# A gated attention and MLP kernel: the first block's projections as plain fp32 products

## The chip, the core and the metric

The kernel runs on one core of one Trainium2 chip. The core has five engines that work at the same time, each through its own list of instructions in order: TensorE (PE, with its weight loads shown as PEld), VectorE (DVE), ScalarE (ACT), GpSimd (POOL) and SyncE (SP, which here only issues transfers). They wait for each other through semaphores. The metric is the device time of one execution in microseconds (us). Three runs before the change took 1068.99, 1069.96 and 1070.19 us, so the median is 1069.96 us.

## The reference: what is computed

For 2048 tokens of width 448 the result is `g * a + (1 - g) * b`. The gate `g` is a sigmoid of one product per token. `a` is attention with 16 query heads of width 28 that share one key head and one value head. `b` is a two-part mixer: a layernorm, a product with `w1`, gelu, four groups of channels shifted by +1, -1, +2 and -2 tokens, a product with `w2` added to `x`, and then a second layernorm with an MLP through `w3` and `w4`.

```
q = (x @ wq).reshape(B, S, H, Dh).transpose(0, 2, 1, 3);  k = x @ wk;  v = x @ wv
p = softmax(einsum("bhqd,bkd->bhqk", q, k) * Dh ** -0.5);  a = merge(p @ v) @ wo
h = gelu(layernorm(x) @ w1);  x1 = x + shifted(h) @ w2
b = x1 + gelu(layernorm(x1) @ w3) @ w4
```

Everything is float32.

## The kernel before

The 448 channels are held as three chunks of 128 and one of 64 rows (`chunks` on the host also repeats the last 64 rows in the upper half of the fourth chunk). The 2048 tokens are four blocks of 512.

**Split products.** A float32 product on TensorE is written in this kernel as several products of a rounded type (`fp32r`, `F32R` in the code). Each operand `a` is split into `ah`, its rounded copy, and `al = a - ah`. `proj` then adds `wh*ah`, `wh*al` and `wl*ah` for three chunks; for the fourth, whose lower part fills the spare 64 rows, it adds two products: 11 matmuls of 512 columns for one output tile. `split_w` makes the two halves of a weight and `split_a` those of an activation: a copy on ACT and subtractions on DVE, or on POOL where `eng` says so.

**Stages.** Stage 1 (`s1`, up to about 105 us) makes keys and values of all blocks (`stage_kv`, `stage_v`), the queries of the first block's head groups 0 and 1 (`stage_q`), and the first half of the mixer (`ln1_begin` and `ln1_tile`, `stage_w1`, `stage_w2`). Stage 2 (up to about 425 us) is the MLP. Stage 3 is attention, bounded by exponentials on ACT together with TensorE, and the output product. The change touches stage 1 only.

**Layernorm.** `layernorm_stats` takes four DVE statistics (`bn_stats`, `bn_aggr`) of a block and then, on POOL, adds epsilon and raises to the power -0.5. `layernorm_tile` normalizes 128 tokens on DVE, repeats the last 64 channels with a POOL copy, transposes four 128x128 pieces on TensorE into one of two `tp` tiles, and splits the result with `split_a`.

**Order.** TensorE's order is that of the program text. The order on the other engines is found by a scheduler when the kernel is built, and is then fixed. Stage 1 begins with 30 small matmuls (`warm`) that only occupy TensorE, then keys and values of block 0, query group 0, the value transposes, query group 1, layernorm of block 0 and `stage_w1(0)`. `stage_w1(b)` has four steps `m` of 112 output channels; between them it transposes layernorm tiles of block `b+1`. Each step ends in two gelus on ACT and a subtraction on POOL (`hh`, `hf`, `hl`).

**Transfers.** SP issues the loads in order: block 0 of the transposed input (`xkv_0`, two halves), two groups of `wq`, block 0 of `x` (`x1`), `w1`, block 1 of `x`, `xkv_1`, `w2`, blocks 2 and 3 of `x`. The six copies of the first queries into their stacked tile (`qs`, `q_evac`) follow on the same queue. `xkv` tiles, `w1raw` and `w2raw` share three buffers (`raw`).

Of the kernel before, what the change touches and what calls it, by code (L numbers as in the profile page):

```python
# [15 lines left out]
P = 128  # L16
# [24 lines left out]
def gated_mix_kernel(  # L41
# [30 lines left out]
    gi = keep.tile([P, NT], F32, name="gi")  # L72
    epst = keep.tile([P, 4], F32, name="epst")
# [4 lines left out]
    nc.gpsimd.memset(powt, -0.5)  # L78
    nc.gpsimd.memset(vext, 0.0)
# [16 lines left out]
    for _ in range(30):  # L96
        nc.tensor.matmul(wps[:, 0:256], warm[:, 0:P], warm, start=True, stop=True)
# [22 lines left out]

    def layernorm_stats(pool, b):
        mv = pool.tile([P, 4, 2], F32, tag="mv", bufs=2, name=f"mv_{pool.name}_{b}")
        rs = pool.tile([P, 4], F32, tag="rs", bufs=2, name=f"rs_{pool.name}_{b}")
        for t in range(4):
            st = pool.tile([P, 6], F32, tag="st", bufs=4, name=f"st_{pool.name}_{b}_{t}")
            nc.vector.bn_stats(st, x1[:, 4 * b + t, :])
            nc.vector.bn_aggr(mv[:, t, :], st)
        nc.gpsimd.tensor_tensor(rs, mv[:, :, 1], epst, ALU.add)
        nc.gpsimd.tensor_tensor(rs, rs, powt, ALU.pow)
        return mv, rs  # L130

    def layernorm_tile(pool, tp_of, b, t, mv, rs, ah, al):
        xt = x1[:, 4 * b + t, :]
        xn = pool.tile([P, 512], F32, tag="xn", bufs=3, name=f"xn_{pool.name}_{b}_{t}")
        nc.vector.tensor_scalar(xn[:, 0:D], xt, mv[:, t, 0:1], rs[:, t:t + 1],
                                op0=ALU.subtract, op1=ALU.mult)
        nc.gpsimd.tensor_copy(xn[:, D:512], xn[:, 384:D])
        tp = tp_of(f"tp_{pool.name}_{b}_{t}").rearrange("p (c n) -> p c n", c=4)
        for c in range(4):
            nc.tensor.transpose(tp[:, c, :], xn[:, c * P:(c + 1) * P], ident)  # L140
        cols = slice(t * P, (t + 1) * P)
        split_a(tp, ah[:, :, cols], al[:, :, cols])
# [60 lines left out]
    with tc.tile_pool(name="s1b", bufs=1) as s1b, \  # L203
# [6 lines left out]
        xraw, xact = {}, {}  # L210
# [10 lines left out]
        nc.scalar.dma_start(kvraw, wkv)  # L221
        xraw[0] = s1.tile([P, 4, 512], F32, tag="raw", bufs=3, name="xkv_0")
        for c in (0, 2):
            nc.sync.dma_start(xraw[0][:, c:c + 2, :], xT[:, c:c + 2, 0:512])
        wqraw = s1.tile([P, 4, 256], F32, name="wq01raw")
        nc.sync.dma_start(wqraw, wq[:, :, 0:256])
        load_x1(0)
        w1raw = s1.tile([P, 4, 512], F32, tag="raw", bufs=3, name="w1raw")[:, :, 0:D]
        nc.sync.dma_start(w1raw, w1)
        load_x1(1)  # L230
        load_x(1)
        w2raw = s1.tile([P, 4, 512], F32, tag="raw", bufs=3, name="w2raw")[:, :, 0:D]
        nc.sync.dma_start(w2raw[0:C, :, :], w2.rearrange("(q p) n -> p q n", p=C))
        load_x1(2)
        load_x1(3)

# [6 lines left out]
        wqh = s1.tile([P, 4, 256], F32R, name="wq01h")  # L243
        wql = s1.tile([P, 4, 256], F32R, name="wq01l")
        hh, hl, acts = {}, {}, {}

        def stage_kv(b):
            ah = s1.tile([P, 4, 512], F32R, tag="ah", bufs=2, name=f"ahk_{b}")
            al = s1.tile([P, 3, 512], F32R, tag="al", bufs=2, name=f"alk_{b}")
            if b == 0:  # L250
                for c in range(4):
                    nc.scalar.copy(ah[:, c, :], xraw[b][:, c, :])
                    if c < 3:
                        nc.vector.tensor_sub(al[:, c, :], xraw[b][:, c, :], f32(ah)[:, c, :])
                    else:
                        nc.vector.tensor_sub(ah[64:128, c, :], xraw[b][64:128, c, :], f32(ah)[64:128, c, :])
            else:
                split_a(xraw[b], ah, al)
            xact[b] = (ah, al)
            cols = slice(512 * b, 512 * b + 512)  # L260
            ps = max_tile(f"kv_{b}")[0:64, :]
            proj(ps, kvh, kvl, ah, al)
            nc.scalar.copy(kS[0:32, cols], ps[0:32, :])
            nc.scalar.copy(kS[32:64, cols], ps[0:32, :])
            nc.vector.tensor_sub(kS[64:96, cols], ps[0:32, :], f32(kS)[0:32, cols])
            vT = s1b.tile([32, 512], F32, tag="vT", bufs=1, name=f"vT_{b}")
            nc.scalar.copy(vT, ps[32:64, :])
            return vT
# [9 lines left out]
        def stage_q(u):  # L278
            ps = mm_tile(f"q_{u}")
            proj(ps, wqh[:, :, u * P:(u + 1) * P], wql[:, :, u * P:(u + 1) * P], *xact[0])  # L280
            q_of[u] = keep.tile([P, 4, 512], F32R, name=f"qs_{u}", tag=f"qs{u}", bufs=1)
            q_evac(s1, u, ps, q_of[u])

        def ln1_begin(b):
            ah = s1.tile([P, 4, 512], F32R, tag="ah", bufs=2, name=f"ah1_{b}")
            al = s1.tile([P, 3, 512], F32R, tag="al", bufs=2, name=f"al1_{b}")
            acts[b] = (ah, al, *layernorm_stats(s1, b))
# [5 lines left out]
        def stage_w1(b):  # L293
# [4 lines left out]
            for m in range(4):  # L298
                ps = mm_tile(f"h_{b}_{m}")
                proj(ps[0:C, :], w1h[:, :, m * C:(m + 1) * C], w1l[:, :, m * C:(m + 1) * C], *acts[b][0:2])  # L300
                if b + 1 < NB:
                    ln1_tile(b + 1, m)
# [27 lines left out]
        split_w(kvraw, kvh, kvl)  # L330
        vT = stage_kv(0)
        split_w(wqraw, wqh, wql, nc.gpsimd)
# [6 lines left out]
        split_w(w1raw, w1h, w1l, nc.gpsimd)  # L339
        stage_w1(0)  # L340
        nc.scalar.copy(w2h[0:C], w2raw[0:C])
        nc.gpsimd.tensor_tensor(w2l[0:C], w2raw[0:C], f32(w2h)[0:C], ALU.subtract)
# [466 lines left out]
```

## Time and profile before

| | |
|---|---|
| median of three runs | 1069.96 us (1068.99 to 1070.19) |
| the profiled execution | 1067.96 us, of which 1066.2 us are the span of its instructions |
| TensorE busy | 1040.3 us (98%), 5610 records |
| ScalarE busy | 673.5 us (63%) |
| VectorE busy | 258.6 us (24%) |
| GpSimd busy | 146.1 us (14%) |
| chain that ended last | 92% TensorE, 2% VectorE, 2% transfers |

The profile shows one execution. Rows of the timeline have a start, a duration, an engine, a line of the kernel, the operation and its tiles, and in brackets how long the engine had been idle and who released it. A table of windows gives for each stretch of time the busy time of each engine with its number of instructions, then the granted TensorE clock as a share of full speed, the share of the transfer engines and GB/s. Matmuls overlap, so a busy TensorE is not TensorE at its peak. Tile names in the profile leave numbers out: `h` is an output of `stage_w1`, `kv` of `stage_kv`, `q` of `stage_q`, `tp_s` a transposed layernorm tile of stage 1, `al` and `ah` its two halves.

### The profile page before, as it was taken

Reading aid. Unit: us, or ns where it says so; the run is one execution under the profiler, and the core shown is the slowest. Engines: PE = TensorE matmul, PEld = TensorE weight load, DVE = VectorE, ACT = ScalarE, POOL = GpSimd, SP = SyncE. Lnnn points to the kernel's source line nnn. Section 1 sums busy time; section 2 is a strip of 40 time slices with the busy share of each in tenths; the row PEclk is TensorE's granted clock in tenths of the full one; section 3 lists DMA queues with packets and bytes.
Section 4 is the critical chain, followed back from the end, with each engine's and each line's share of the span. In section 5 each row is a group of like instructions: output and inputs, shape, how many; then the busy total and the mean of one; then the engine's idle time right before and its main releaser. Section 6 shows DMA issues by size and latency. Waiting matters only on the chain.

```text
span 1066.2 us, 13945 instructions
## 1 busy us (share of the span) xinstructions
PE 1040.3 (98%) x5610; PEld 679.5 (64%) x5610; DVE 258.6 (24%) x528; ACT 673.5 (63%) x1318; POOL 146.1 (14%) x175
## 2 busy tenths in 40 slices
PE   7999989999999999999999999999999999999996
PEld 4787878888888887454554555554655555555442
DVE  6734862411412212301110110120110210111102
ACT  5444462222222223798888888889888888888873
POOL 5622200200200202602000002020002010000100
PEclk8899999999999999999999999999999999999998
DMA  9501330000000001323211202220202220202001
GB/s 312 133 1 37 112 111 1 1 1 1 1 1 1 1 1 61 132 32 70 32 18 15 31 19 41 39 31 3 39 10 41 39 31 2 40 21 30 10 2 38
DMA packets 30541, 41.15 MB, mean 39 GB/s; under 512 B 8004, under 2 KB 20100, under 8 KB 30340
## 3 DMA queue, kind: packets, MB, share of 16 engines
q1 hardware_dynamic: 30324, 40.04, 16.2%
q8 instruction: 46, 0.75, 0.3%
q14 instruction: 27, 0.22, 0.1%
q10 hardware_dynamic: 144, 0.13, 0.0%
HBM read 23.28 MB, written 3.67 MB: 25 GB/s over the span
## 4 chain that ended last, share of the span: by engine, by line
PE 92%; DVE 2%; DMA 2%; ACT 1%; POOL 1%; issue 1%; SPq 0%; POOLq 0%; DVEq 0%; ACTq 0%
PE s L662 27%; PE pv L624 22%; PE acc L418 4%; PE acc L419 4%; PE acc L420 4%; PE g L115 4%; PE g L116 4%; PE g L117 4%; PE q L502 3%; PE m L166 2%; PE wo L559 1%; PE wo L557 1%; PE g L119 1%; PE wo L555 1%; PE g L118 1%; PE h L116 1%
## 5 line engine op out<-in xcount | busy, mean ns | idle before, releaser
L664 ACT ACTIVATE p<-s 128x512 f32<-128x512 f32 x1024 | 517.6, 630 | 99.7 <-PE s L662 99.4
L662 PE MATMUL s<-qs,kS 98*128 98x512 f32 x1024 | 343.5, 420 | 1.4 <-ACT p L664 0.7
L662 PEld LDWEIGHTS s<-qs,kS 98*128 98x128 f32 x1024 | 181.7, 189 | 168.3 <-ACT p L664 126.2
L624 PE MATMUL pv<-p,vext 128*32 128x512 f32 x2048 | 247.5, 601 | 0.0
L408 ACT ACTIVATE gh<-g 128x512 fp32r<-128x512 f32 x56 | 33.6, 599 | 175.0 <-PE g L119 174.9
L624 PEld LDWEIGHTS pv<-p,vext 128*32 128x32 f32 x2048 | 53.7, 109 | 107.5 <-issue 100.1
L410 DVE TENSOR_TENSOR gl<-gf,gh 128x512 fp32r<-128x512 f32 x56 | 38.7, 692 | 183.8 <-ACT gf L409 183.8
L418 PE MATMUL acc<-w4h,gh 128*128 128x448 f32 x224 | 82.8, 370 | 0.0
L419 PE MATMUL acc<-w4l,gh 128*128 128x448 f32 x224 | 82.0, 366 | 0.0
L420 PE MATMUL acc<-w4h,gl 128*128 128x448 f32 x224 | 81.7, 365 | 0.0
L167 DVE TENSOR_REDUCE mr<-m 128x4 f32<-128x512 f32 x64 | 44.2, 691 | 146.8 <-PE m L166 146.1
L115 PE MATMUL g<-ah,w3h 128*128 128x512 f32 x168 | 66.6, 396 | 3.7 <-ACT gf L409 3.7
L116 PE MATMUL g<-al,w3h 128*128 128x512 f32 x168 | 66.3, 395 | 0.0
L117 PE MATMUL g<-ah,w3l 128*128 128x512 f32 x168 | 66.3, 394 | 0.0
L547 POOL CAST onh<-on 128x512 fp32r<-128x512 f32 x15 | 9.2, 614 | 415.0 <-DVE on L544 228.9
L520 DVE SCALAR_TENSOR_TENSOR good<-rt,good 128x16 f32<-128x16 f32 x15 | 2.6, 175 | 190.9 <-DMA rt<-o 190.9
L418 PEld LDWEIGHTS acc<-w4h,gh 128*128 128x128 f32 x224 | 42.2, 188 | 4.9
L419 PEld LDWEIGHTS acc<-w4l,gh 128*128 128x128 f32 x224 | 42.2, 188 | 4.9
L420 PEld LDWEIGHTS acc<-w4h,gl 128*128 128x128 f32 x224 | 42.0, 188 | 3.6
L166 PEld LDWEIGHTS m<-kS,qs 96*128 96x128 f32 x256 | 38.4, 191 | 6.3 <-DVE mr L167 1.2
L115 PEld LDWEIGHTS g<-ah,w3h 128*128 128x128 f32 x168 | 31.7, 188 | 9.9 <-ACT gf L409 4.1
L563 DVE SCALAR_TENSOR_TENSOR ot<-wo,gg,x 128x448 f32<-128x448 f32 x16 | 10.9, 681 | 108.0 <-PE wo L559 107.9
(204 smaller groups left out, 1134.9 us busy)
## 6 DMA issues: line engine op xcount, KB each, us to landing
qs<-qh SPq DMA_DIRECT2D x32, 256.0 KB
qs<-ql SPq DMA_DIRECT2D x16, 256.0 KB
xq<-in_xT_dram SPq DMA_DIRECT2D x4, 1024.0 KB
x<-in_x_dram SPq DMA_DIRECT2D x4, 896.0 KB
w3raw<-in_w_dram SPq DMA_DIRECT2D x7, 512.0 KB
out_dram<-ot SPq DMA_DIRECT2D x16, 224.0 KB
w4raw<-in_w_dram SPq DMA_DIRECT2D x7, 448.0 KB
xkv<-in_xT_dram SPq DMA_DIRECT2D x3, 1024.0 KB
```

The costliest lines, as they stand in the source:

```text
L115: nc.tensor.matmul(ps, wh[:, c, :], ah[:, c, :], start=(c == 0), stop=False)
L116: nc.tensor.matmul(ps, wh[:, c, :], al[:, c, :], start=False, stop=False)
L117: nc.tensor.matmul(ps, wl[:, c, :], ah[:, c, :], start=False, stop=False)
L166: nc.tensor.matmul(ps[:, j, :], q_of[u][0:96, j, t * P:(t + 1) * P], kS[0:96, 0:MK], start=True, stop=True)
L167: nc.vector.reduce_max(mx_of[u][:, :, t], ps, axis=AX.X)
L410: nc.vector.tensor_sub(gl, gf, f32(gh))
L418: nc.tensor.matmul(ps, gh[:, tok], w4h[i][:, k, :], start=(f == 0), stop=False)
L419: nc.tensor.matmul(ps, gh[:, tok], w4l[i][:, k, :], start=False, stop=False)
L420: nc.tensor.matmul(ps, gl[:, tok], w4h[i][:, k, :], start=False, stop=(f == NF - 1))
L624: nc.tensor.matmul(pv[32 * j:32 * j + 32, :], vext[:, kt, :], ps[j], start=(kt == 0), stop=(kt == NT - 1), tile_position=(0, 32 * j))
L662: nc.tensor.matmul(ps, kS[0:98, kt * P:(kt + 1) * P], q_of[u][0:98, j, :], start=True, stop=True)
L664: nc.scalar.activation(p, ps, AF.Exp, scale=SCALE)
```

## The change

In block 0, keys and values, the two query groups and the four steps of `stage_w1(0)` are made by a new `proj32`: four matmuls with both operands plain float32, straight from the loaded tiles. The fourth chunk's weights get zeros in rows 64 to 127 (`kvlast`, the last chunk of `wqraw`, `w1last`), set on DVE, with 64 rows loaded beside them. So block 0 needs no split of `xkv_0`, `wq` or its layernorm tiles; these are copied whole, alternately by ACT and DVE. Blocks 1 to 3 still use split halves, so `w1`, `w2` and the key and value weights are still split, with the subtractions of `w1` and `w2` moved from POOL to DVE. In stage 1 the repeated last 64 channels are normalized a second time on DVE where POOL copied them. The first block's power is taken in two pairs. A gelu on four columns stands at the head of ACT, so its table is loaded there. The warming matmuls go from 30 to 22. The loads of blocks 1 and 2 of `x` and `w2` come ahead of block 3 of `x`, and `xkv_1` comes last of these.

```diff
     gi = keep.tile([P, NT], F32, name="gi")
+    first = keep.tile([P, 4], F32, name="first")
     epst = keep.tile([P, 4], F32, name="epst")
...
     nc.gpsimd.memset(powt, -0.5)
+    nc.scalar.activation(first, powt, AF.Gelu_apprx_tanh)
     nc.gpsimd.memset(vext, 0.0)
...
     wps = misc_tile("warm_ps")
-    for _ in range(30):
+    for _ in range(22):
         nc.tensor.matmul(wps[:, 0:256], warm[:, 0:P], warm, start=True, stop=True)
...
+    def proj32(ps, w, w3, a):
+        for c in range(4):
+            nc.tensor.matmul(ps, w(c) if c < 3 else w3, a[:, c, :], start=(c == 0), stop=(c == 3))
+
     def layernorm_stats(pool, b):
+        pairs = (1, 3) if pool.name == "s1" and b == 0 else (3,)
         mv = pool.tile([P, 4, 2], F32, tag="mv", bufs=2, name=f"mv_{pool.name}_{b}")
...
             nc.vector.bn_aggr(mv[:, t, :], st)
-        nc.gpsimd.tensor_tensor(rs, mv[:, :, 1], epst, ALU.add)
-        nc.gpsimd.tensor_tensor(rs, rs, powt, ALU.pow)
+            if t in pairs:
+                w = slice(t - pairs[0], t + 1)
+                nc.gpsimd.tensor_tensor(rs[:, w], mv[:, w, 1], epst[:, w], ALU.add)
+                nc.gpsimd.tensor_tensor(rs[:, w], rs[:, w], powt[:, w], ALU.pow)
         return mv, rs
...
         xt = x1[:, 4 * b + t, :]
-        xn = pool.tile([P, 512], F32, tag="xn", bufs=3, name=f"xn_{pool.name}_{b}_{t}")
+        xn = pool.tile([P, 512], F32, tag="xn", bufs=4 if pool.name == "s1" else 3, name=f"xn_{pool.name}_{b}_{t}")
         nc.vector.tensor_scalar(xn[:, 0:D], xt, mv[:, t, 0:1], rs[:, t:t + 1],
                                 op0=ALU.subtract, op1=ALU.mult)
-        nc.gpsimd.tensor_copy(xn[:, D:512], xn[:, 384:D])
+        if pool.name == "s1":
+            nc.vector.tensor_scalar(xn[:, D:512], xt[:, 384:D], mv[:, t, 0:1], rs[:, t:t + 1],
+                                    op0=ALU.subtract, op1=ALU.mult)
+        else:
+            nc.gpsimd.tensor_copy(xn[:, D:512], xn[:, 384:D])
         tp = tp_of(f"tp_{pool.name}_{b}_{t}").rearrange("p (c n) -> p c n", c=4)
...
         cols = slice(t * P, (t + 1) * P)
-        split_a(tp, ah[:, :, cols], al[:, :, cols])
+        if al is None:
+            (nc.vector.tensor_copy if t % 2 else nc.scalar.copy)(f32(ah)[:, :, cols], tp)
+        else:
+            split_a(tp, ah[:, :, cols], al[:, :, cols])
...
-        xraw, xact = {}, {}
+        xraw = {}
...
         nc.scalar.dma_start(kvraw, wkv)
+        kvlast = s1.tile([P, 64], F32, name="wkvlast")
+        wqraw = s1.tile([P, 4, 256], F32, name="wq01raw")
+        w1last = s1.tile([P, D], F32, name="w1last")
+        for w in (kvlast, wqraw[:, 3, :], w1last):
+            nc.vector.memset(w[64:128], 0.0)
+        nc.scalar.dma_start(kvlast[0:64], wkv[0:64, 3, :])
         xraw[0] = s1.tile([P, 4, 512], F32, tag="raw", bufs=3, name="xkv_0")
...
             nc.sync.dma_start(xraw[0][:, c:c + 2, :], xT[:, c:c + 2, 0:512])
-        wqraw = s1.tile([P, 4, 256], F32, name="wq01raw")
-        nc.sync.dma_start(wqraw, wq[:, :, 0:256])
+        nc.sync.dma_start(wqraw[:, 0:3, :], wq[:, 0:3, 0:256])
+        nc.sync.dma_start(wqraw[0:64, 3, :], wq[0:64, 3, 0:256])
         load_x1(0)
...
         nc.sync.dma_start(w1raw, w1)
+        nc.sync.dma_start(w1last[0:64], w1[0:64, 3, :])
         load_x1(1)
-        load_x(1)
+        load_x1(2)
         w2raw = s1.tile([P, 4, 512], F32, tag="raw", bufs=3, name="w2raw")[:, :, 0:D]
         nc.sync.dma_start(w2raw[0:C, :, :], w2.rearrange("(q p) n -> p q n", p=C))
-        load_x1(2)
         load_x1(3)
+        load_x(1)
...
         w2l = s1b.tile([P, 4, D], F32R, name="w2l")
-        wqh = s1.tile([P, 4, 256], F32R, name="wq01h")
-        wql = s1.tile([P, 4, 256], F32R, name="wq01l")
         hh, hl, acts = {}, {}, {}
...
         def stage_kv(b):
-            ah = s1.tile([P, 4, 512], F32R, tag="ah", bufs=2, name=f"ahk_{b}")
-            al = s1.tile([P, 3, 512], F32R, tag="al", bufs=2, name=f"alk_{b}")
-            if b == 0:
-                for c in range(4):
-                    nc.scalar.copy(ah[:, c, :], xraw[b][:, c, :])
-                    if c < 3:
-                        nc.vector.tensor_sub(al[:, c, :], xraw[b][:, c, :], f32(ah)[:, c, :])
-                    else:
-                        nc.vector.tensor_sub(ah[64:128, c, :], xraw[b][64:128, c, :], f32(ah)[64:128, c, :])
-            else:
-                split_a(xraw[b], ah, al)
-            xact[b] = (ah, al)
             cols = slice(512 * b, 512 * b + 512)
             ps = max_tile(f"kv_{b}")[0:64, :]
-            proj(ps, kvh, kvl, ah, al)
+            if b == 0:
+                proj32(ps, lambda c: kvraw[:, c, :], kvlast, xraw[0])
+            else:
+                ah = s1.tile([P, 4, 512], F32R, tag="ah", bufs=2, name=f"ahk_{b}")
+                al = s1.tile([P, 3, 512], F32R, tag="al", bufs=2, name=f"alk_{b}")
+                split_a(xraw[b], ah, al)
+                proj(ps, kvh, kvl, ah, al)
             nc.scalar.copy(kS[0:32, cols], ps[0:32, :])
...
             ps = mm_tile(f"q_{u}")
-            proj(ps, wqh[:, :, u * P:(u + 1) * P], wql[:, :, u * P:(u + 1) * P], *xact[0])
+            w = slice(u * P, (u + 1) * P)
+            proj32(ps, lambda c: wqraw[:, c, w], wqraw[:, 3, w], xraw[0])
             q_of[u] = keep.tile([P, 4, 512], F32R, name=f"qs_{u}", tag=f"qs{u}", bufs=1)
...
             ah = s1.tile([P, 4, 512], F32R, tag="ah", bufs=2, name=f"ah1_{b}")
-            al = s1.tile([P, 3, 512], F32R, tag="al", bufs=2, name=f"al1_{b}")
+            al = s1.tile([P, 3, 512], F32R, tag="al", bufs=2, name=f"al1_{b}") if b else None
             acts[b] = (ah, al, *layernorm_stats(s1, b))
...
                 ps = mm_tile(f"h_{b}_{m}")
-                proj(ps[0:C, :], w1h[:, :, m * C:(m + 1) * C], w1l[:, :, m * C:(m + 1) * C], *acts[b][0:2])
-                if b + 1 < NB:
-                    ln1_tile(b + 1, m)
+                w = slice(m * C, (m + 1) * C)
+                if b == 0:
+                    proj32(ps[0:C, :], lambda c: w1raw[:, c, w], w1last[:, w], f32(acts[0][0]))
+                    for t in ((), (0, 1), (2, 3), ())[m]:
+                        ln1_tile(1, t)
+                else:
+                    proj(ps[0:C, :], w1h[:, :, w], w1l[:, :, w], *acts[b][0:2])
+                    if b + 1 < NB:
+                        ln1_tile(b + 1, m)
                 hf = s1.tile([P, 512], F32, tag="hf", bufs=2, name=f"hf_{b}_{m}")
...
-        split_w(kvraw, kvh, kvl)
         vT = stage_kv(0)
-        split_w(wqraw, wqh, wql, nc.gpsimd)
         stage_q(0)
...
             ln1_tile(0, t)
-        split_w(w1raw, w1h, w1l, nc.gpsimd)
+        split_w(w1raw, w1h, w1l)
         stage_w1(0)
         nc.scalar.copy(w2h[0:C], w2raw[0:C])
-        nc.gpsimd.tensor_tensor(w2l[0:C], w2raw[0:C], f32(w2h)[0:C], ALU.subtract)
+        nc.vector.tensor_tensor(w2l[0:C], w2raw[0:C], f32(w2h)[0:C], ALU.subtract)
+        split_w(kvraw, kvh, kvl)
         stage_w1(1)
```

## The prediction

> **What bounds the kernel now.** I read the page first. TensorE is busy for 98% of the span and makes 92% of the chain that ended last. Its clock, however, is lower in the early slices, so a table of windows over stage 1 came second, cut where the granted clock changes (windows 3.41 us apart).
>
> ```profile
> PE 92%; DVE 2%; DMA 2%; ACT 1%; POOL 1%; issue 1%; SPq 0%; POOLq 0%; DVEq 0%; ACTq 0%
> PEclk8899999999999999999999999999999999999998
> ```
>
> ```profile
> 8.52:11.93 3.41, 1.58 (x7) 0.62 (x5) 0.94 (x3) 2.69 (x5) 2.24 (x2) 1.00 1.05 396
> 11.93:15.35 3.42, 3.42 (x9) 2.25 (x7) 2.44 (x8) 1.79 (x2) 1.64 (x6) 0.50 1.06 383
> 18.76:22.17 3.41, 1.34 (x11) 0.94 (x9) 3.37 (x9) 1.61 (x3) 2.83 (x4) 1.00 1.07 248
> 22.17:25.58 3.41, 2.08 (x8) 1.03 (x6) 2.04 (x7) 1.74 (x3) 1.30 (x3) 0.50 1.05 366
> 25.58:29.00 3.42, 2.29 (x6) 1.57 (x6) 3.13 (x4) 2.40 (x2) 2.62 (x3) 0.50 1.08 211
> 60.00:105.00 45.00, 45.00 (x216) 34.94 (x216) 17.44 (x30) 17.80 (x28) 10.74 (x19) 1.00 0.03 9
> ```
>
> Two things are to be seen. After a window with 1.58 or 1.34 us of TensorE work the clock is 0.50, and it stays there after 2.08 and 2.29 us; only a full window restores it. And from 60 to 105 us TensorE has no gap, at clock 1.00. So what counts is the time at which block 1's `stage_w1(1)` starts; what follows is tied to TensorE's progress. The chain to that start is third:
>
> ```profile
> 2.48 8.60 DMA x<-in_x_dram
> 11.11 1.15 DVE st_s L126 x2
> 24.71 1.04 POOL rs_s L129
> 26.94 0.77 PE h L116
> 27.71 0.43 PE h L117
> 42.12 0.57 DVE al L110
> 42.73 0.49 PE h L116
> 43.22 0.23 PE h L117
> ```
>
> Block 0 of `x` lands at 11.1 us, DVE and POOL work until TensorE gets `h` going at 26.94, first at half clock (0.43 us a matmul, against 0.23), and `stage_w1(1)` is held until 42.73 by the low half `al`.
>
> **The new matmul's price.** The only plain float32 product in the trace is attention's (L624). The program has 1024 of them.
>
> ```profile
> L624 PE MATMUL pv<-p,vext x2048: 592/592/1061, 427.0 to 1051.1; 128*32 128x512 f32 x187
> 603.88 1.92 PE L624 MATMUL pv<-p,vext 128*32 128x512 f32 x16
> 604.33 0.13 PEld L624 LDWEIGHTS pv<-p,vext 128*32 128x32 f32 x4 [0.30 <-issue]
> 604.76 0.13 PEld L624 LDWEIGHTS pv<-p,vext 128*32 128x32 f32 x4 [0.30 <-issue]
> ```
>
> So each is two records, and groups of four (side by side in 32 columns) follow every 0.43 us. One matmul costs 0.855 us, `proj32` four of them, 3.42 us, against 11 x 0.23 = 2.53 us for `proj`. Below, if one record sufficed (as for a transpose, 0.11 us for 128 columns), 1.72 us. Above, no row has two-record matmuls on 128 columns; were the load of 0.19 us (128 columns, L116) exposed at each of 8 records, 4.94 us. I take 3.42, because the loads above run ahead of their matmuls.
>
> **The change, part by part.** All times are estimates from rows of the profiled execution, 1067.96 us long (span 1066.2 and 1.76 around it), which is 2.0 us below the median.
>
> *Start.* 22 warming matmuls at 0.171 us end at 4.8 us instead of 6.2. Without a split, `kv` starts there (`xkv_0` landed near 4.6 and 6.1) and lasts to 8.3; the first queries, whose weights land near 8.5, to about 11.9, the value transposes to 12.3, the second queries to 15.7. TensorE's waits for POOL's `wq` half (1.2 us) and ACT's copies go. The three zero fills on DVE stand at 1 to 2 us, when DVE is idle; TensorE's need for them and for the extra 16 KB load, behind the table load on ACT (1.28 us), comes at 7.4 us or later. If that cover failed, `kv` would end later by the excess, with some 1.9 us of slack before it is felt (below).
>
> *Transfers.* SP issues two more loads early, about 0.6 us each; 48 KB less stand ahead of block 0 of `x`, 0.12 us at 390 GB/s. I take its landing at 11.0; bounds 10.9 to 11.6. By bytes at 390 GB/s, `w1` lands at 13.4, `x` blocks 1 and 2 at 16 and 18.4, `w2` at 20.5, `x` block 3 at 23 and `xkv_1` near 26. `xkv_1` now waits for the second queries (its buffer), and the six `qs` copies queue behind it on SP; ACT casts `xkv_1` at 55.7 now, and `qs` is first read in stage 2, so both are free up to 25 us of lateness.
>
> *Layernorm of block 0, now DVE's chain.* Four statistics from 11.0 end at 13.35 (0.59 each); value copies, a query half and two aggregates to 14.55; the first power pair is done by then, the second by 15.9 (POOL: 0.27 + 1.02 and gaps; for two columns perhaps less). Four tiles at 0.45 to 0.51 plus the second operation of 64 columns, bounded by 0.15 (4 columns, L276) and 0.27 (112, L275), taken at 0.15: 0.65 each, to 17.2. POOL's copies of 0.28 and their waits go. Then comes `w1`'s low half, moved from POOL (3.30 us) to DVE: from 768 columns in 0.95 and 896 in 1.07, 1344 take 1.5 us, to 18.7. In DVE's list this stands ahead of the two copies for `stage_w1(0)`, as does the second query half (0.68). The copies have no row of their own; ACT's takes 0.58, DVE's subtraction from the same memory 0.68, which I take: 20.8. Here `stage_w1(0)` starts, against 26.94. TensorE itself was ready about 1.9 us earlier.
>
> *`stage_w1(0)`.* 4 x 3.42 + 4 x 0.44 of transposes = 15.4 us at full clock. In the window from 18.76 to 22.17 TensorE would be busy for some 1.4 us, as in those after which the clock fell; it then is half to 25.58, which costs 1.7 us. End: 20.8 + 15.4 + 1.7 = 37.9. The split path took 14.1 us from 26.94 to 41.0, so TensorE's step itself becomes longer.
>
> *Block 1's layernorm.* On DVE: the rest of `w1` to 21.2, statistics to 24.2, power to 25.6, four tiles to 28.2, `w2`'s low half (1792 columns: 1.95 us, from POOL's 4.01) to 30.2. The first transposes come after two steps, 20.8 + 6.84 + 1.7 = 29.3 to 30.2; ACT copies them by 30.6 and 31.2; four subtractions (0.57 and 0.29 in pairs) end at 32.4, block 2's statistics at 34.6, power at 36.05, a tile at 36.55, and the remaining low halves at 38.1, when `stage_w1(1)` gets going. DVE ends 0.2 us behind TensorE.
>
> *No price of their own.* ACT's second table load (1.28 us at 26.7) lay beside TensorE's first step until 31.4; ACT's `w2` copy, 22.2 at the latest, precedes the first gelu near 26. The rest of the repeated 64 channels (blocks 2, 3) adds 8 x 0.15 us to DVE, busy for 17.4 of 45 us there. The first load of stage 2 still waits for `stage_w1(3)` on TensorE, so it moves with it.
>
> *Sum:* 38.1 against 42.73 is -4.6 us: 1063.4 for the profiled execution, 1065.4 us on the median.
>
> **A rule weighed against the clock rows.** In the rows the clock falls after pauses of only 0.6 and 1.2 us within one window (8.9 to 11.6 us). The Trainium skill, "TensorE: Matmul & The Clock Gate", section "Why this matters for your kernels", asks for no gap above about 3 us between bursts. The pauses here would be about 1.5 us, so by that rule the clock would stay full, and the sum would be the first rival's -5.3 us instead of -4.6. The trace speaks against it.
>
> **Rivals.**
> *The clock stays full.* Then TensorE is done at 36.2, and DVE, whose first transposes come 0.6 us earlier at most, holds it to 37.4: -5.3, 1064.7. For it: 1.4 us of work is not far below the unknown bound.
> *Half clock for a second window*, or DVE slower by about as much: 1.7 us more, -2.9, 1067.1. For it: the windows of 2.08 and 2.29 us stayed low. Against: TensorE has no pause once started.
> *Gain lost.* A later landing (0.6), dearer small DVE operations (13 x 0.1) and the dearer copy together leave about -1.5, 1068.5.
> *Slower: the full-width float32 matmul is dearer.* With d us more for each `proj32`, four stand on the path and three ahead of it, with 1.9 us of slack: -4.6 + 4d + (3d - 1.9). It decides at d = 0.93, a record of 0.54 us instead of 0.43. With exposed loads (d = 1.5) it gives +4.0, 1074.0. For it: no such record is in the trace. Against: the loads that run ahead.
>
> **How the numbers follow.** The forecast, 1065.4 with its own range 1064.5 to 1066.4, has 0.50; clock full 0.12; second window 0.14; gain lost 0.08; slower 0.16. About 0.2% (2.1 us) is what a measurement can tell from no change; the first three are faster by more: 0.76, same 0.08, slower 0.16. Three runs differ by 1.2 us. The range leaves out the slower case and a little beyond the full clock: 1063.5 to 1069.5.
>
> **What would show it.** `kv` at 4.8 us; records of `proj32` every 0.43 us, two for each matmul; the first `h` near 20.8 and clock 0.50 for one window after it; the first `al` product of block 1 at 38.1, and equal spacing from there on. It is wrong if records come 0.54 us apart or more, if block 0 of `x` lands after 12, or if stage 2's first loads wait for something that does not move.

## The result, and the profile after

The changed kernel takes 1065.83 us (median of seven runs, 1062.28 to 1067.31); seven runs of the kernel before, beside them, have a median of 1069.2 us. The ratio is 0.9967 with a 95% interval of 0.9955 to 0.9978, so the change is worth 3.5 us (2.4 to 4.8; all differences below are ratios times 1069 us). The forecast was 1065.4 us and -4.6 us. The profiled execution took 1066.31 us with a span of 1064.5.

First the two lines of the page, the shares of the chain that ended last and the granted clock by slices:

```profile
PE 93%; DVE 3%; ACT 1%; POOL 1%; DMA 1%; issue 1%; POOLq 0%; DVEq 0%; SPq 0%; ACTq 0%
PEclk9999989999999999999999999999999999999998
```

The low clock of the first two slices is gone, and a low slice has come in the sixth, near 135 us. Some windows, cut where this execution's clock changes (busy time and number of instructions of PE, PEld, DVE, ACT, POOL, then the clock):

```profile
19.97:23.38 3.41, 2.62 (x9) 1.27 (x10) 3.19 (x8) 0.00 (x0) 0.00 (x0) 1.00 1.06 262
37.03:40.45 3.42, 1.68 (x7) 0.90 (x6) 3.30 (x8) 1.08 (x2) 1.99 (x4) 1.00 0.96 316
129.20:132.61 3.41, 1.22 (x6) 0.68 (x4) 3.41 (x10) 3.33 (x6) 0.18 (x1) 1.00 0.05 20
132.61:136.02 3.41, 2.08 (x5) 1.71 (x6) 3.17 (x6) 2.80 (x5) 1.21 (x2) 0.50 0.64 194
136.02:139.43 3.41, 3.41 (x9) 2.72 (x9) 2.06 (x4) 1.39 (x4) 0.00 (x0) 0.50 0.35 109
```

Stage 1 keeps the full clock. The fall comes behind TensorE's pause at the start of stage 2. The new matmul, by its source line (minimum, median and maximum in ns), and the main pieces of the chain of waits to `stage_w1(1)`, others between them left out:

```profile
L125 PE MATMUL h<-ah,w1raw x24: 592/592/683, 21.3 to 35.9; 128*112 128x512 f32 x24
```

```profile
1.05 4.87 PE warm_ps L99 x22
5.92 3.80 PE kv L125 x8
13.72 3.64 PE q L125 x8
17.38 0.59 ACT qh L163
17.97 0.49 ACT ah L156
20.54 0.69 DVE ah L156
26.50 1.08 DVE xn_s L147
29.52 1.93 DVE w2l L362
36.52 1.27 DVE xn_s L144
38.70 0.57 DVE al L112
39.31 0.49 PE h L118
```

`stage_w1(0)` starts at 21.29 us (before: 25.04, and 26.94 for its first product with `al`), and the first product of block 1 that needs `al` at 39.31 (before: 42.73), so 3.4 us are gained there. The first product of stage 2 starts at 125.23 (before: 128.37), still -3.1. At the first product behind stage 2's pause and its low clock, `g` of the fourth step, it is 141.55 against 143.89, -2.3. By the first product of attention it is -1.8 (418.77 against 420.57), and -2.3 at TensorE's last transpose (1055.22 against 1057.51). The spans differ by 1.7, since 0.6 more pass at the very end. So the two profiled executions differ by less than the medians do.

### The profile page after: what moved, and what is told of

It reads as the page before. It is cut to its first block, busy times and chain, and to the rows that moved or that the text cites. A ratio compares the mean times of both kernels' runs of the same rounds, so it can differ in the third digit from the quotient of the medians.

```text
span 1064.5 us, 13873 instructions
## 1 busy us (share of the span) xinstructions
PE 1041.8 (98%) x5581; PEld 673.1 (63%) x5581; DVE 261.7 (25%) x540; ACT 667.3 (63%) x1309; POOL 132.6 (12%) x155
## 4 chain that ended last, share of the span: by engine, by line
PE 93%; DVE 3%; ACT 1%; POOL 1%; DMA 1%; issue 1%; POOLq 0%; DVEq 0%; SPq 0%; ACTq 0%
PE s L683 27%; PE pv L645 22%; PE acc L439 4%; PE acc L440 4%; PE acc L441 4%; PE g L117 4%; PE g L118 4%; PE g L119 4%; PE q L523 3%; PE m L182 2%; PE wo L580 1%; PE g L121 1%; PE wo L578 1%; PE g L120 1%; PE wo L576 1%; PE h L118 1%
```

## The experiments

Each was timed beside the kernel before on its own chip; the changed kernel's 0.9967 is the mark to hold them against.

### Undoing one part: the w1 product

```diff
-            al = s1.tile([P, 3, 512], F32R, tag="al", bufs=2, name=f"al1_{b}") if b else None
+            al = s1.tile([P, 3, 512], F32R, tag="al", bufs=2, name=f"al1_{b}")
...
-                if b == 0:
-                    proj32(ps[0:C, :], lambda c: w1raw[:, c, w], w1last[:, w], f32(acts[0][0]))
-                    for t in ((), (0, 1), (2, 3), ())[m]:
-                        ln1_tile(1, t)
-                else:
-                    proj(ps[0:C, :], w1h[:, :, w], w1l[:, :, w], *acts[b][0:2])
-                    if b + 1 < NB:
-                        ln1_tile(b + 1, m)
+                proj(ps[0:C, :], w1h[:, :, w], w1l[:, :, w], *acts[b][0:2])
+                if b + 1 < NB:
+                    ln1_tile(b + 1, m)
```

(Block 0's activations get their low half again, and the transposes of block 1 their old places, one tile behind each step.)

> Only block 0's w1 product goes back to the split form (its activations get their low half on DVE again, 11 fast matmuls a step); keys, values, queries, loads and all else stay as in the changed kernel. Theory (DVE's list sets the start of stage_w1(1)): four low halves of 0.86 us and w1's 64 rows (0.61 us) stand ahead of TensorE in place of two copies of 0.68, so stage_w1(0) starts near 24 instead of 21.3, its step takes 11.9 us at full clock, and the first al product of block 1 comes near 41.3 instead of 39.3: about 2 us slower than the changed kernel, 1.4 faster than before. Rival (TensorE's own step sets it): four plain products cost TensorE 3.6 us more than four split ones, so without them the al product comes near 38 and the kernel is 1 us or more faster than the changed one.

Measured: ratio 1.0071 (1.0056 to 1.0087), 11.1 us slower than the changed kernel. The direction is the theory's, the size is not. Its timeline shows what was added:

```profile
29.11 1.09 POOL L323 TENSOR_TENSOR hl<-hf,hh 112x512 fp32r<-112x512 f32 x1 [12.68 <-ACT hf L322]
30.16 0.20 POOL L137 TENSOR_TENSOR rs_s<-mv_s,epst 128x4 f32<-128x4 f32 x1
31.48 0.51 DVE L144 TENSOR_SCALAR xn_s<-x,mv_s,rs_s 128x448 f32<-128x448 f32 x1 [2.46 <-POOL rs_s L138]
47.82 0.77 PE L118 MATMUL h<-al,w1h 128*112 128x512 f32 x1 [2.43 <-DVE al L112]
```

In POOL's list the gelu subtraction now stands ahead of block 1's power, and waits for a product that is late. DVE stands still for 2.5 us, the clock falls three times (0.50 from 23.8 to 27.2, from 30.6 to 37.5 and from 47.7 us), and the `al` product comes at 47.82. The rival has fallen: without the plain products TensorE isn't early. How much of the loss is the split form, how much POOL's new order and how much the place of the transposes is not separated.

### Undoing one part: keys, values and queries

```diff
-            proj32(ps, lambda c: wqraw[:, c, w], wqraw[:, 3, w], xraw[0])
+            proj(ps, wqh[:, :, u * P:(u + 1) * P], wql[:, :, u * P:(u + 1) * P], *xact[0])
...
+        split_w(wqraw, wqh, wql, nc.gpsimd)
         stage_q(0)
```

(`stage_kv` likewise; for space, `xn` has three buffers instead of four.)

> Only the keys, values and queries of block 0 go back to the split form (with POOL making wq's low half); the w1 product stays plain and the loads keep the new order. Theory (block 0's layernorm on DVE sets the start of stage_w1(0), TensorE is ready earlier): TensorE is done with the second queries near 18.7 instead of 17.2, the layernorm's transposes come up to 1.5 us later, and the al product of block 1 at 39.3 to 40.3: 0 to 1 us slower than the changed kernel, 2.4 to 3.4 faster than before. Rival (the early start of keys and queries carries the gain): 2.5 us or more slower than the changed kernel.

Measured: ratio 1.0017 (1.0004 to 1.0029), 5.3 us slower than the changed kernel. The rival's size came true. TensorE waited for POOL's half of `wq` (1.23 us) and for ACT's `vT` (2.09), the clock was 0.50 from 15.8 to 19.2, the layernorm's transposes began at 20.26 (17.18 in the changed kernel), and `stage_w1(0)` at 24.39. The 3.1 us came through whole, so the slack of 1.9 us ahead of it, on which the forecast counted, was not there. More was lost behind it:

```profile
26.59 1.99 DVE L368 TENSOR_TENSOR w2l<-w2raw,w2h 112x1792 fp32r<-112x1792 f32 x1
26.76 1.89 POOL L137 TENSOR_TENSOR rs_s<-mv_s,epst 128x4 f32<-128x4 f32 x1 [11.36 <-DVE mv_s L134]
29.70 1.09 POOL L332 TENSOR_TENSOR hl<-hf,hh 112x512 fp32r<-112x512 f32 x1
29.77 1.27 DVE L144 TENSOR_SCALAR xn_s<-x,mv_s,rs_s 128x448 f32<-128x448 f32 x1 [1.18 <-POOL rs_s L138]
43.27 0.48 PE L118 MATMUL h<-al,w1h 128*112 128x512 f32 x1 [2.15 <-DVE al L112]
```

POOL's tiny addition (0.20 us elsewhere) takes 1.89 us beside DVE's `w2l`, and DVE's normalizing 1.27 us in place of 0.51 beside POOL's subtraction.

### Undoing one part: the low halves of w1 and w2 back on POOL

```diff
-        split_w(w1raw, w1h, w1l)
+        split_w(w1raw, w1h, w1l, nc.gpsimd)
...
-        nc.vector.tensor_tensor(w2l[0:C], w2raw[0:C], f32(w2h)[0:C], ALU.subtract)
+        nc.gpsimd.tensor_tensor(w2l[0:C], w2raw[0:C], f32(w2h)[0:C], ALU.subtract)
```

> Only the low halves of w1 and w2 go back from DVE to POOL (3.3 and 4.0 us there). Theory (exclusion between DVE and POOL): stage_w1(0) starts 1.5 us earlier, near 19.8, since the copies no longer stand behind w1's low half; but a normalizing operation of block 1 stands still for up to 4 us beside w2's low half, as one did before (4.21 us for two), POOL's own subtractions queue behind it, and the al product comes at 40 to 41: about 1 us slower than the changed kernel. Rival (the move to DVE is a burden on the engine that is the bound): DVE has 4.2 us less work, the al product comes at 37.5 to 38 behind TensorE's step, and the kernel is 1.5 us faster than the changed one.

Measured: ratio 1.0018 (1.0005 to 1.0031), 5.5 us slower than the changed kernel. The rival has fallen, and the theory was too mild:

```profile
15.78 3.03 POOL L106 TENSOR_TENSOR w1l<-w1raw,w1h 128x1344 fp32r<-128x1344 f32 x1
15.86 3.21 DVE L144 TENSOR_SCALAR xn_s<-x,mv_s,rs_s 128x448 f32<-128x448 f32 x1
26.80 3.97 POOL L362 TENSOR_TENSOR w2l<-w2raw,w2h 112x1792 fp32r<-112x1792 f32 x1
26.86 4.15 DVE L144 TENSOR_SCALAR xn_s<-x,mv_s,rs_s 128x448 f32<-128x448 f32 x1 [0.89 <-POOL rs_s L138]
```

Both times DVE starts 0.06 to 0.08 us after POOL and ends 0.24 to 0.26 us after it. It hits block 0 too, which the expectation had overlooked: `stage_w1(0)` starts at 23.70, not at 19.8, at half clock, and the first `al` product that the trace shows is at 44.45.

### Undoing one part: the order of the loads

```diff
         load_x1(1)
-        load_x1(2)
+        load_x(1)
...
-        load_x1(3)
-        load_x(1)
+        load_x1(2)
+        load_x1(3)
```

> Only the order of the loads goes back: the second block of keys' input before w2, the third block of x behind w2. Theory (the order carries nothing by itself): what DVE needs for block 1 keeps its place, w2 lands near 23.5 as before, since its bytes stand behind about as many; the first al product of block 1 stays at 39.3 within 0.5 and the time within 0.5 us of the changed kernel. Rival (the order is part of the gain): w2 now waits for the second queries (its buffer) and, with it, all that stands behind it in SP's queue; ACT's cast of w2 comes later than 25 and stands ahead of the first gelu, and the kernel is 1 to 2 us slower than the changed one.

Measured: ratio 0.9961 (0.9948 to 0.9975), 0.6 us faster than the changed kernel and not to be told from it. So no part of the gain is seen to hang on the order; the rival has fallen. The trace differs more than was expected: the `al` product is at 36.82, 2.5 us earlier. Of this, 1.0 comes from the start (`stage_w1(0)` at 20.32): the warming matmuls doubled their pace at 4.2 us, while in the changed kernel's profile all 22 had the slow one, and `kv` began 0.7 earlier. The other 1.5 come from DVE's first normalizing of block 2, which stands only behind block 1's low halves. At the first product of stage 2 (124.30 against 125.23) only 0.9 us of that is left.

### DVE and POOL: one shared resource

This is the changed kernel's timeline of the two engines:

```profile
26.19 1.34 POOL L328 TENSOR_TENSOR hl<-hf,hh 112x512 fp32r<-112x512 f32 x1 [0.15 <-ACT hf L327]
26.50 1.08 DVE L147 TENSOR_SCALAR xn_s<-x,mv_s,rs_s 128x64 f32<-128x64 f32 x1
29.44 2.01 DVE L362 TENSOR_TENSOR w2l<-w2raw,w2h 112x1792 fp32r<-112x1792 f32 x1
30.58 1.83 POOL L328 TENSOR_TENSOR hl<-hf,hh 112x512 fp32r<-112x512 f32 x1 [3.04 <-ACT hf L327]
36.45 1.09 POOL L328 TENSOR_TENSOR hl<-hf,hh 112x512 fp32r<-112x512 f32 x1
36.52 1.27 DVE L144 TENSOR_SCALAR xn_s<-x,mv_s,rs_s 128x448 f32<-128x448 f32 x1 [0.89 <-POOL rs_s L138]
38.54 1.09 POOL L328 TENSOR_TENSOR hl<-hf,hh 112x512 fp32r<-112x512 f32 x1 [0.31 <-ACT hf L327]
38.70 0.56 DVE L112 TENSOR_TENSOR al<-tp_s,ah 128x384 fp32r<-128x384 f32 x1
```

The engine that comes second is held until the first is done: DVE's 64 columns take 1.08 us instead of 0.31, its 448 columns 1.27 instead of 0.51, POOL's subtraction 1.83 instead of 1.09. `al`, whose first input is TensorE's output tile and only the second an ordinary tile, is not held (0.56 us beside the subtraction at 38.54). The Trainium skill, "SBUF — State Buffer", section "Who interferes with whom", has this as a rule: the only ports of GpSimd are a pair that it shares with DVE under an exclusive lock. A DVE operation with two inputs from SBUF contends with a GpSimd operation that reads SBUF, one with at most one input from there doesn't, and scaling operations can enter a mode that takes the pair for a whole instruction. These rows agree (1.27 us for a scaling in place of 0.51, and 0.56 for `al`). The test takes the subtractions of block 0 away and fills their output with zeros instead, 1.81 us on POOL at 4.7 us:

```diff
+            if b == 0:
+                nc.gpsimd.memset(f32(hl[b])[0:C, :, 2:514], 0.0)
...
-                nc.gpsimd.tensor_tensor(hl[b][0:C, m, 2:514], hf[0:C, :], f32(hh[b])[0:C, m, 2:514],
-                                        ALU.subtract)
+                if b > 0:
+                    nc.gpsimd.tensor_tensor(hl[b][0:C, m, 2:514], hf[0:C, :], f32(hh[b])[0:C, m, 2:514],
+                                            ALU.subtract)
```

> Leaves out a part: the low half of block 0's gelu (four subtractions on POOL of 1.09 us) is not computed but left at zero. Theory (DVE's normalizing operation and POOL's subtraction exclude each other): the two operations of DVE that took 1.08 and 1.27 us beside such a subtraction take 0.31 and 0.51, the low halves of block 1 are done 1.5 us earlier, and the first al product comes at 37.8 instead of 39.3, behind TensorE's own step (about 37): 1 to 1.5 us faster than the changed kernel. Rival (the long durations are waits of another kind, or TensorE's step is what holds it): the durations stay above 1 us, or the al product stays at 39 or later, and the time within 0.3 us of the changed kernel.

Measured: ratio 0.9952 (0.9935 to 0.9968), 1.6 us faster than the changed kernel by the medians of the comparison, though the intervals overlap. The trace is clear:

```profile
26.76 0.31 DVE L147 TENSOR_SCALAR xn_s<-x,mv_s,rs_s 128x64 f32<-128x64 f32 x1
36.01 0.51 DVE L144 TENSOR_SCALAR xn_s<-x,mv_s,rs_s 128x448 f32<-128x448 f32 x1 [0.89 <-POOL rs_s L138]
38.05 0.48 PE L118 MATMUL h<-al,w1h 128*112 128x512 f32 x1 [0.53 <-DVE al L112]
```

Both durations fall as said, and `al` comes at 38.05 in place of 39.31. The next kernel does all the work, but later:

```diff
         stage_w1(0)
+        nc.gpsimd.tensor_copy(hl[0][0:1, :, 2], f32(acts[1][1])[0:1, 2, 508:512])
+        for m in range(4):
+            low_half(0, m)
```

(`low_half` is the subtraction, taken out of `stage_w1(0)`; `hf` has four buffers. The copy's four elements are overwritten by the subtractions.)

> The four subtractions of block 0's gelu on POOL are all computed, but held back until DVE has made block 1's low halves (a copy of four elements that they wait for); their inputs get four buffers. Theory (exclusion between DVE and POOL): the same as with them left out: DVE's two long operations take 0.31 and 0.51 us, the first al product comes at 38.0, and the kernel is 1 to 1.6 us faster than the changed one; what the subtractions now lock out (block 2's normalizing, 39 to 44 us) has more than 15 us of slack. Rival (leaving the work out, not its place, made that kernel faster): the al product stays at 39, or the time within 0.4 us of the changed kernel.

Measured: ratio 0.9988 (0.9977 to 1.0), 2.2 us slower than the changed kernel. Here the theory's mechanism held and its price failed:

```profile
37.56 0.48 PE L118 MATMUL h<-al,w1h 128*112 128x512 f32 x1 [0.53 <-DVE al L112]
49.40 0.63 PE L153 MATMUL tp_s<-ident,xn_s 128*128 128x128 f32 x4 [3.32 <-DVE ah L113]
```

`al` is there at 37.56, but the four subtractions in a row hold DVE's normalizing of block 2, later block 3's power and normalizing come late, and DVE's `al` of block 2 stands behind them; TensorE's transposes need the `tp` buffer that it frees. The slack was under 10 us, not 15. So only two moments were moved, the first two subtractions behind block 1's last normalizing, the others behind block 2's first:

```diff
+                elif m == 2:
+                    hold(1, 3)
+                    low_half(0, 0)
+                    low_half(0, 1)
...
+                    if b == 1 and m == 0:
+                        nc.gpsimd.tensor_copy(hl[0][0:1, 2:4, 2], xn_of[2, 0][0:1, 0:2])
+                        low_half(0, 2)
+                        low_half(0, 3)
```

(`hold` is such a copy from the end of a normalized tile.)

> All four subtractions of block 0's gelu are computed on POOL, but only two moments are moved: the first two wait until block 1's last normalizing operation is done (near 29), the third until block 2's first is (near 36), through copies of a few elements. Theory (holding all four back failed because they then locked out block 2's and 3's normalizing, whose transposes have little slack): no normalizing operation before 38 lasts longer than 0.55 us, the first al product comes at 38.0 or earlier, TensorE doesn't wait for 3 us near 49, and the kernel is 1 to 1.6 us faster than the changed one, like the one that left them out. Rival (any subtraction beside this stage's DVE work costs its time somewhere): the time stays within 0.5 us of the changed kernel.

Measured: ratio 0.9952 (0.9939 to 0.9965), as with the work left out.

```profile
37.82 0.49 PE L118 MATMUL h<-al,w1h 128*112 128x512 f32 x1 [0.56 <-DVE al L112]
47.26 0.63 PE L153 MATMUL tp_s<-ident,xn_s 128*128 128x128 f32 x4 [0.90 <-DVE ah L113]
```

The 3.3 us wait has shrunk to 0.90, which is still part of the gain given back: in the profile, 1.5 us at `al` are 0.4 at the start of `stage_w2(0)` (50.62 against 51.02) and 0.3 at stage 2. DVE's normalizing at 35.76 takes 0.51 us again. That DVE and POOL hold each other is shown by the durations in four kernels. That moving the work gains 1.6 us in the whole time is not: the interval touches the changed kernel's, and the profile accounts for less.

### The clock behind stage 2's pause

```diff
+                if b == 0 and f == 2:
+                    fps = misc_tile("fill_ps")
+                    for _ in range(20):
+                        nc.tensor.matmul(fps[:, 0:256], warm[:, 0:P], warm, start=True, stop=True)
                 gs[f] = w3_part(b, f)
```

> Adds 20 idle matmuls of the warming kind (about 0.11 us each at full clock) into TensorE's pause at the start of stage 2; they end before the pause does. Theory (the changed kernel's clock falls after this pause, and the before kernel's only later): the clock keeps 1.00 behind the pause, the step there takes 2.5 us instead of 4.9 at half clock, and the kernel is 0.9 to 2.4 us faster than the changed one in its profile, 0.5 to 1 us in the median, since not every execution has the fall. Rival (the fall has nothing to do with this pause): the clock still falls there, and the time is within 0.3 us of the changed kernel or slower.

Measured: ratio 0.9941 (0.9928 to 0.9954), 2.8 us faster than the changed kernel, more than the 0.5 to 1 expected of the median. The timelines of the changed kernel and of this one:

```profile
133.94 0.80 PE L117 MATMUL g<-ah,w3h 128*128 128x512 f32 x1 [3.52 <-ACT gf L430]
134.53 0.63 PE L118 MATMUL g<-al,w3h 128*128 128x512 f32 x1
```

```profile
130.26 2.36 PE L457 MATMUL fill_ps<-warm 128*128 128x256 bf16 x20
133.81 0.50 PE L117 MATMUL g<-ah,w3h 128*128 128x512 f32 x1 [1.20 <-ACT gf L430]
134.15 0.39 PE L118 MATMUL g<-al,w3h 128*128 128x512 f32 x1
```

The pause ends at the same time, but the products behind it follow at full clock, and the fourth step starts at 138.90 instead of 141.55. This lead of 2.6 us is unchanged at attention's first product (416.15 against 418.77). The profiled executions lie further apart, 1061.29 against 1066.31 us, and most of the rest comes from another place. In the changed kernel TensorE then waits for POOL's low half of the queries, and its clock is 0.50 behind the wait, from 436.4 to 439.8 us:

```profile
435.67 0.50 PE L523 MATMUL q<-alq,wqh 128*128 128x512 f32 x1 [1.39 <-POOL alq L509]
```

With the idle matmuls the clock was 0.50 earlier, from 422.7 to 426.1, and this product came at 433.16 without a wait; the lead grew to 4.2 us. The wait of 1.4 us is in the traces of six kernels, the one before among them, and missing in seven. What decides this isn't shown, so whole times of single profiles are not to be compared to within 1.6 us.

A fall of the clock that comes in some executions only may also explain the spread: the changed kernel's runs fall into 1065.3 to 1067.3 us with a mean clock of 0.991 to 0.993 and 1062.3 to 1062.5 us with 0.995, while with the idle matmuls all five lie between 1061.1 and 1062.2 us at 0.996 or 0.997. Only one execution of the changed kernel has a trace, so this is not shown. The same edit in the kernel before:

> The kernel before, with the same 20 idle matmuls in TensorE's pause at the start of stage 2. Theory (each kernel loses what its clock falls there: 2.5 us in the changed kernel's profile, 1.6 in that of the kernel before): 1 to 1.7 us faster than the kernel before, ratio 0.9985 to 0.999; held against the changed kernel with the same idle matmuls (0.9941) the change is then worth 4.5 to 5 us, about the 4.6 that were forecast. Rival (the idle matmuls help for another reason, for instance a faster array afterwards): the same 2.5 to 3 us as in the changed kernel, ratio 0.9972 to 0.9977.

Measured: ratio 0.9989 (0.9977 to 1.0), 1.2 us faster. That is within the theory's range, but the interval reaches from no gain to the rival's 2.5 us. In its trace the clock stays full at the pause, and a lag of 2.1 us behind the kernel before, at the first product of stage 2 (130.44 against 128.37), shrinks to 1.3 at the fourth step (145.21 against 143.89), so 0.8 us is gained there. With the idle matmuls on both sides the change is worth 0.9941 against 0.9989, some 5.1 us; the two intervals together leave about 1.9 us of doubt, so this is not separable from either 3.5 or 4.6.

### The pause itself, and a faster version

In the changed kernel ACT loads gelu's table a second time in the pause (1.28 us at 130.53), because the scheduler put the gate's small exponential at 107.24. This kernel makes it wait for stage 2's last result:

```diff
-        nc.scalar.activation(gg, gz, AF.Exp, scale=-1.0)
+        gy = s3.tile([P, NT], F32, name="gy")
+        nc.vector.scalar_tensor_tensor(gy, x1[:, NT - 1, 0:NT], 0.0, gz, op0=ALU.mult, op1=ALU.add)
+        nc.scalar.activation(gg, gy, AF.Exp, scale=-1.0)
```

> The small exponential of the gate (128 x 16) is made to wait for stage 2's last result, so that ACT doesn't load its table at 105.9 and gelu's again at 130.5, in the middle of TensorE's pause at the start of stage 2. Theory (that second load of 1.28 us stands in the chain that ends the pause): the pause, 3.5 us in the changed kernel, is 1.3 us shorter, and the kernel 1.2 us faster than the changed one, up to 2.1 if the clock then doesn't fall. Rival (the weights' loads and casts end the pause): the pause stays above 3 us and the time within 0.4 us of the changed kernel.

Measured: ratio 1.0079 (1.0066 to 1.0092), 12 us slower than the changed kernel. Stage 2 did gain more than expected (the fourth step at 138.02 instead of 141.55, with one pause of 1.55 us), and attention lost it:

```profile
417.54 11.03 POOL L618 TENSOR_SCALAR x<-x,gi 128x448 f32<-128x448 f32 x7 [7.78 <-issue]
433.50 8.29 POOL L618 TENSOR_SCALAR x<-x,gi 128x448 f32<-128x448 f32 x6
441.77 3.40 POOL L511 TENSOR_TENSOR alq<-xq,ahq 128x1536 fp32r<-128x1536 f32 x1
445.23 0.80 PE L525 MATMUL q<-alq,wqh 128*128 128x512 f32 x1 [14.09 <-POOL alq L511]
```

The scalings of `x1`, which wait for the gate, now stand in POOL's list ahead of the queries' low half. Moving them behind it mends that:

```diff
+        nc.vector.scalar_tensor_tensor(gi, f32(xact[0][1])[:, 2, 0:NT], 0.0, gi, op0=ALU.mult, op1=ALU.add)
         for n in range(NT):
             nc.gpsimd.tensor_scalar(x1[:, n, :], x1[:, n, :], gi[:, n:n + 1], None, op0=ALU.mult)
```

> The gate's exponential again after stage 2, and now the 16 scalings of x1 on POOL, which use its result, wait until POOL has made the first low half of attention's queries. Theory (the late exponential shortened stage 2's start by 3.5 us against the changed kernel, and lost 14 us since those scalings, 1.4 us each, stood ahead of the queries' low halves in POOL's list): TensorE's wait of 14 us near 445 is gone, and the kernel is 2.5 to 3.5 us faster than the changed one, 1059 to 1061 us beside 1068.5 of the kernel before. Rival (attention's start needs the exponential itself or its table late): a wait of several us stays between 415 and 450, and the kernel is no faster than the changed one.

Measured: 1061.6 us, ratio 0.9926 (0.9914 to 0.9939), 4.4 us faster than the changed kernel, whose interval it doesn't touch, where 2.5 to 3.5 were expected. The wait of 14 us is gone (so is the 1.4 us that the changed kernel had there), the pause in stage 2 is this one, and the clock doesn't fall behind it:

```profile
138.32 0.50 PE L117 MATMUL g<-ah,w3h 128*128 128x512 f32 x1 [1.53 <-ACT gf L430]
```

It has the lowest ratio here, though its interval overlaps that of the kernel with idle matmuls. With the two moved moments of the subtractions added:

> Both changes that gained, together: the subtractions of block 0's gelu moved in two places, and the gate's exponential and the scalings of x1 late. Theory (they act at different places, stage 1 and the start of stage 2): 1 to 1.6 us faster than the kernel with the late exponential alone, ratio to the kernel before 0.991 to 0.9917, near 1060 us. Rival (what stage 1 gains is taken back by the later wait for stage 2's weights): the first al product comes at 38.0, but the ratio stays at 0.9926 within 0.0004.

Measured: ratio 0.9931 (0.9917 to 0.9944). `al` comes at 37.88, and the time can't be told from that of the late exponential alone: the rival's outcome. Only 0.3 us of the 1.4 is left at the start of stage 2 (126.22 against 126.53), as above.

Not undone by themselves were the early gelu, the power in two pairs, the second normalizing in place of POOL's copy, and the number of warming matmuls.

## Why the prediction was right

The time and the sign were right, by a path of which some terms were wrong in both directions. That 1065.83 lies so close to 1065.4 is in part luck: the gain was 1.1 us smaller than forecast, and the median of the kernel before was 0.8 us lower over seven runs (1069.2) than over the three that the forecast started from (1069.96).

- *The price of the plain matmul* was right: records follow every 0.43 us, two for each, with weights of 112 columns, 128 for the queries, loaded beside them (the second step's eight run from 24.81 to 28.24 us). With it fell the one rival of the other side: break-even was 0.54 us a record.
- *Start.* `kv` began at 5.92, not at 4.8. The failed term is the warming matmul at 0.171 us, a mean over two paces: in the kernel before the first 20 start 0.21 us apart (1.05 to 5.08) and the last ten 0.11, in the changed kernel all 22 are 0.21 apart. So dropping eight saved little. The keys' subtraction then held DVE's statistics to 11.66 (taken: 11.0; `x` itself landed by 10.83, as another kernel shows, inside the bounds).
- *Layernorm of block 0, the moves to DVE*: four tiles at 0.66 to 17.57, `w1l` 1.55 and copies 0.68 as priced; start of `stage_w1(0)` 21.29 for 20.8. But DVE's list didn't set this start alone, and "TensorE itself was ready about 1.9 us earlier" failed. The chain runs from the second queries through ACT, where their cast `qh` (17.38) stands ahead of the first copy of a transposed tile, to the last transposes; DVE had been idle for 0.22 us when it took the last copy at 20.54. So the late start of `kv` counted in full, as the kernel with the loads' old order shows from the other side. (The 26.94 of the forecast was the first product with `al`; the split step itself began at 25.04. Its sum goes by 42.73 and doesn't change.)
- *The clock in stage 1* was forecast to fall for one window, at 1.7 us. It stayed full: TensorE's queries ended later, so the window that holds the pause had 2.62 us of work, not 1.4. The first rival's condition came true and its price, 1064.7 from DVE at 37.4, did not.
- *DVE's list to the `al` product*: 39.31 for 38.1. The step that failed is "four tiles to 28.2" and "a tile at 36.55": 0.8 us more each, the two held operations. The list began 0.55 later; the low halves, statistics and small steps were 0.9 shorter, mostly since TensorE's transposes weren't late. The kernel with the subtractions left out came to 38.05 without them. The row that would have told it was in the trace before, two normalizings of 4.21 us together beside POOL's `w2l`.
- *What follows moves with it*: true from 39.31 to the start of stage 2 (3.4 and 3.1 us). It failed behind stage 2's pause: there the kernel before already lost some clock, and the changed one lost more in its profile, which takes 0.8 us of the gain. The forecast had no term for this; the two kernels with idle matmuls put the loss at 2.8 and 1.2 us by the medians, 2.6 and 0.8 by the traces.
- *The lost-gain and second-window rivals*: the gain was in fact cut, from 4.6 to 3.4 us at `al`, by a term none of them had.

The rule weighed in the forecast, no gap above about 3 us (the Trainium skill, "TensorE: Matmul & The Clock Gate", section "Why this matters for your kernels"), did better than the forecast made of it: pauses up to 1.74 us in the changed kernel's stage 1 kept the clock, and the pause of 3.52 us lost it. But the kernel before lost it behind pauses of 0.6 and 1.2 us, and the kernel with all four subtractions late kept it over a pause of 3.53 us, which fell into two windows:

```profile
132.19:135.61 3.42, 1.53 (x7) 0.94 (x5) 3.42 (x10) 3.30 (x5) 0.49 (x2) 1.00 0.13 49
135.61:139.02 3.41, 1.78 (x8) 1.47 (x9) 3.16 (x7) 2.78 (x6) 1.21 (x2) 1.00 0.53 160
```

The work in a window of 3.41 us doesn't divide the rows either. Windows with 1.22, 1.34 and 1.58 us of TensorE work lost the clock and ones with 1.68 and 2.62 kept it, but in other kernels 1.47 us kept it (keys, values and queries split, from 39.6 us) and 1.78 lost it (`w1` product split, from 20.4). At attention's start it fell behind a window that was full (idle matmuls, from 419.3). Nor does it take a full window to win it back, as the forecast read: 3.06 us did (keys, values and queries split, from 138.6). So the one window of half clock in stage 1 was forecast from a rule that doesn't hold, and what decides a fall stays open.

## What to carry to other kernels

Price an operation on DVE or POOL by what runs beside it on the other one: look in the trace for the same operation with two durations. When work leaves an engine, read the whole list of every engine again, since an order found by a scheduler can put a waiting instruction ahead of the one on the path; undoing any one of three parts here cost more than the whole change had gained, though each edit also let the scheduler find another order. And a gain early in a kernel is only kept if the pauses behind it, and the clock after them, are carried along in the sum.

## What was not expected of the hardware

A tiny operation can be held as long as a large one: POOL's addition on four columns took 1.89 us beside a two-input DVE operation of 1.99, and DVE's 64 columns took 1.08. A clock fall of one or two windows at a single pause moves what follows by up to 2.6 us, and twenty matmuls of no use, 2.4 us long, in a pause of 3.5, took that away. But with about the same pause one kernel's profile had the fall and another's had not.
